# A fused attention and token-mixing kernel: other load queues, a narrower packed tile, fixed buffers, and a new order of all steps

## The chip, the cores and the metric

The kernel runs on one core of one Trainium2 chip. The metric is device time in microseconds (us), the median over runs; lower is better. The core has five instruction queues: TensorE (PE, its weight loads shown apart as PEld), VectorE (DVE), ScalarE (ACT), GpSimd (POOL) and SyncE (SP). Each executes its own instructions strictly in order and waits on semaphores for the others. Transfers are done by 16 DMA engines, fed from a queue of SP, a queue of ACT (both "hardware" queues in the profile) and a queue of POOL (the "software" queue, the only one here that casts fp32 to bf16 on the way).

## The reference

Two attentions in a row and then a token mixer. `B, H, S, Dh = 8, 8, 576, 64`, and 32 packed queries `p` per head.

```python
def sm_attn(qq, kk, vv):
    s = scale * np.matmul(qq, kk.transpose(0, 1, 3, 2))
    s = s - np.max(s, axis=-1, keepdims=True)
    a = np.exp(s)
    a = a / (np.sum(a, axis=-1, keepdims=True) + 1e-09)
    return np.matmul(a, vv)
p_packed = sm_attn(p, k, v)                 # 32 packed rows per head
out = sm_attn(q, p_packed, p_packed)        # every token attends to the 32 rows
x = out.transpose(0, 2, 1, 3).reshape(B, S, H * Dh)
W_tok = scale2 * np.einsum('bsd,btd->bst', x @ w_q, x @ w_k)   # 64 hidden columns
mixed = np.einsum('bst,btd->bsd', W_tok, x)
return np.maximum(mixed, 0.0) @ w_out
```

Inputs and output are fp32; q, k and v are 9.4 MB each.

## The kernel before

The work is cut into 8 batches and each batch into some 30 named steps. A string `ORDER`, written out by hand (or by a planner outside of the file), lists all steps of all batches in one sequence, with `@V`, `@A` or `@P` for the engine that does a step (DVE, ACT, POOL) and `=2,3` for the PSUM banks. A step's instructions are appended to its engine's queue in this sequence, so `ORDER` fixes the order on each engine, but two engines run apart as far as data allow. A place late in `ORDER` does not hold an instruction back if its engine has nothing else to do.

The steps of batch b, with the line of their instructions:

- `LD.kb`, `LD.qb`, `LD.vb`: the casting loads on POOL's queue (L181, L185, L177; v is loaded in two halves). `LD.K0`, `LD.K1` (batch 0's k in fp32, on SP, L163), `LD.P0` to `P3` and `LD.W0`, `W1` (on ACT, L167, L170), `LD.O` (w_out, POOL, L172).
- `KC`, `PC`, `WC` cast k of batch 0, p and the weights on chip (L131, L133, L135 for ACT, POOL, DVE). `KT`, `PX`, `TE`, `PT`, `QV` are transposes in blocks on DVE, all through one helper (L223), told apart by their tiles kT, pT, e, ppT, qT.
- First attention: `S1` scores (PE, L261), `X1` exponential (ACT, L266, tile e1T), `TE`, `PV` (PE, L282, reads v_sb and e), `RC` reciprocal (DVE, L287), `PP` (DVE, L294): divides by the row sum and multiplies by a mask, giving the packed rows pp.
- Second attention: `PT` transposes pp to ppT, `S2` scores (PE, L339), `X2` (ACT, L344), `RS` row sums (DVE, L354), `RR` (DVE, L359), `AM` multiplies (POOL or DVE, L365), `AT` transposes on PE (L374), `AE` evicts them (tile aT).
- Mixer: `QK` multiplies ppT with the weights wqk (PE, L306), `QKE` evicts (tile pqk); `WKQ` (L396, L401), `WE`, `GM` (L422), `GE`, `Y` (L432), `YE`, `MX` (L446) and `MR` (L452, the last 64 tokens), `RL`, `RLF`, `RLR` relu evictions (L457, L459), `OT` (PE, L491) the product with w_out, four matmuls each, `OE`, `OEF` evictions into tiles o and o_rem, `ST`, `STF` stores on SP (L496; L511 for o_rem, the last rows of two batches together).
- `WARM.n` are n matmuls on a zero tile (L535); they compute nothing that is used.

Tiles come from pools (`inpool` 4 buffers, `bpool` 3, `epool` 2, `opool` 10). Each casting load also waits for the one that stands eight DMAs ahead of it on POOL's queue, as they share eight semaphores.

The pp tile of before has 2 x 2 x 128 columns: for each pair of heads the rows stand four times, and the mask leaves one head in each. `PT` turns all of it, so that `QK` can use 128 rows at once.

Of the kernel before, what the change touches and what calls it, by code (L numbers as in the profile page):

```python
# [7 lines left out]
NL, NB, NO, NE = 4, 3, 10, 2  # L8

ORDER = """  # L10
SET.warm LD.P0 LD.P1 LD.P2 LD.P3 LD.W0 LD.W1 LD.K0 LD.k1 LD.K1 SET.mask@V KC.0@V SET.v0@V LD.v0 PC@V
LD.q0 KT.0.0@V KC.1@A SET.v3@V PX@V KT.0.1@V SET.v1@V WARM.27=0 S1.0=0,1,2,3 SET.idf@V KT.1.2@V
SET.aff@P X1.0.1@A LD.k2 WC.0@P SET.aT0@V TE.0.1@V WARM.4=4 S1.1=4,5,6,7 LD.v1 SET.v2@V X1.1.1@A
X1.0.0@A LD.q1 X1.1.0@A TE.0.0@V LD.v2 SET.aT1@V TE.1.1@V WARM.6=2 PV.0.0=2,3 LD.k4 PV.0.1 QV.0.1@V
WC.1@P QV.0.0@V LD.q2 RC.0.1@V RC.0.0@V PP.0.1@V QV.0.2@V PP.0.0@V PT.0@V LD.k3 KT.2.2@V WARM.9=6
S2.0.2=6,7 S2.0.3=0,1 X2.0.2@A X2.0.3@A SET.idb@V TE.1.0@V RS.0.4@V WARM.5=4 PV.1.0=4,5 LD.O PV.1.1
QK.0=2 RC.1.0@V RC.1.1@V RR.0.4@V S1.2=6,7,0,1 PP.1.0@V AM.0.2@P PP.1.1@V AM.0.3@P PT.1@V WARM.1=3
AT.0.2=3 QV.1.1@V AE.0.2@A QK.1=4 X1.2.0@A SET.aT2@V QV.1.0@V QKE.0@A X1.2.1@A QV.1.2@V WARM.2=5
S2.1.3=6,7 LD.v3 QKE.1@A TE.2.1@V S2.1.2=2,3 AT.0.3=5 X2.1.2@A TE.2.0@V X2.1.3@A AE.0.3@V WARM.1=0
PV.2.0=0,1 RS.1.4@V WKQ.0.0=2,3 WKQ.0.2 WKQ.0.1 PV.2.1 WE.0.2@A RR.1.4@V KT.4.2@V AM.1.2@P WARM.1=4  # L20
GM.0=4 AM.1.3@P GE.0@V RC.2.1@V RC.2.0@V WARM.1=6 Y.0=6 PP.2.1@V S1.4=2,3,4,5 YE.0@V PP.2.0@V
X1.4.1@A MX.0.0=6,7 LD.q3 QV.2.0@V MX.0.1=0,1 RL.0.0@A AT.1.3=4 PT.2@V LD.v4 QV.2.1@V AT.1.2=5
X1.4.0@A AE.1.3@V S2.2.3=6,7 RL.0.1@A LD.q4 QV.2.2@V AE.1.2@V S2.2.2=2,3 KT.3.2@V LD.k5 WKQ.1.0=4,5
X2.2.3@A WKQ.1.1 X2.2.2@A WKQ.1.2 S1.3=0,1,6,7 WE.1.2@A RS.2.4@V QK.2=2 X1.3.1@A GM.1=3 LD.q5
OT.0.2=4,5 X1.3.0@A TE.3.1@V GE.1@A OT.0.0=6,7 RR.2.4@V TE.3.0@V OT.0.3 AM.2.2@V AM.2.3@V OT.0.1
LD.k6 OE.0.1@A TE.4.1@V AT.2.2=3 AT.2.3=0 OE.0.0@A AE.2.2@V Y.1=1 TE.4.0@V PV.3.0=4,5 QKE.2@A YE.1@V
MR.0=6,7 PV.3.1 AE.2.3@V RLR.0@A MR.1=2,3 MX.1.0=6,7 LD.v5 RLR.1@A RC.3.1@V QV.3.1@V WKQ.2.0=0,1
RL.1.0@A MX.1.1=2,3 RC.3.0@V WKQ.2.2 PP.3.1@V WKQ.2.1 PP.3.0@V OT.1.4=6 WE.2.2@A PT.3@V QV.3.2@V
QK.3=7 QV.3.0@V OEF.1.4@A GM.2=4 LD.v6 RL.1.1@V PV.4.0=0,1 ST.1.4 GE.2@A QKE.3@A Y.2=6 PV.4.1 YE.2@V
S2.3.2=4,5 S2.3.3=2,3 RC.4.0@V X2.3.2@A RC.4.1@V PP.4.1@V MX.2.0=6,7 OT.1.2=4,5 PP.4.0@V RL.2.0@A  # L30
QV.4.0@V MX.2.1=0,1 X2.3.3@A QV.4.2@V MR.2=6,7 OT.1.3 PT.4@V QV.4.1@V RLR.2@A RL.2.1@A OT.1.0=2,3
RS.3.4@V OE.1.1@A S2.4.2=6,7 S2.4.3=0,1 OT.1.1 RR.3.4@V X2.4.3@A KT.5.2@V AM.3.3@P OT.2.0=4,5
X2.4.2@A OE.1.0@A RS.4.4@V S1.5=0,1,6,7 OT.2.1 LD.q6 X1.5.0@A AM.3.2@V X1.5.1@A LD.k7 AT.3.3=2
RR.4.4@V QV.5.1@V OE.2.0@A OT.2.2=0,1 AM.4.3@P AE.3.3@V QK.4=3 TE.5.1@V AT.3.2=6 OT.2.3 AE.3.2@A
QKE.4@A KT.6.2@V WKQ.3.0=4,5 AM.4.2@P OE.2.1@A AT.4.3=7 LD.v7 WKQ.3.2 WKQ.3.1 AE.4.3@V AT.4.2=6
S1.6=2,3,0,1 WE.3.2@A AE.4.2@V TE.5.0@V WKQ.4.0=6,7 X1.6.1@A QV.5.0@V GM.3=4 LD.q7 WKQ.4.2 X1.6.0@A
WKQ.4.1 GE.3@V PV.5.0=0,1 TE.6.1@V WE.4.2@A Y.3=5 TE.6.0@V PV.5.1 YE.3@A GM.4=4 RC.5.1@V QV.5.2@V
MX.3.1=2,3 RC.5.0@V GE.4@A MX.3.0=6,7 PP.5.0@V RL.3.1@A PV.6.0=4,5 PP.5.1@V Y.4=0 PT.5@V PV.6.1
RL.3.0@A YE.4@V S2.5.3=2,3 RC.6.1@V RC.6.0@V QK.5=1 PP.6.0@V X2.5.3@A PP.6.1@V OT.3.0=6,7 PT.6@V
QKE.5@A S2.5.2=4,5 QV.6.2@V MX.4.0=2,3 QV.6.1@V MR.3=0,1 X2.5.2@A OT.3.1 RL.4.0@A QV.6.0@V RLR.3@V  # L40
S2.6.2=4,5 RS.5.4@V MX.4.1=2,3 S2.6.3=0,1 X2.6.2@A RL.4.1@A OT.3.4=4 X2.6.3@A RR.5.4@V OT.4.0=2,3
OEF.3.4@V AM.5.3@P OE.3.0@A KT.7.2@V QK.6=5 ST.3.4 ST.1.0 OT.4.1 ST.0.0 ST.1.1 ST.0.1 ST.2.0 ST.3.0
OT.3.2=0,1 RS.6.4@V OE.4.0@A AM.5.2@P AT.5.3=4 QKE.6@A ST.4.0 S1.7=6,7,2,3 ST.2.1 RR.6.4@V AE.5.3@V
AT.5.2=5 AM.6.3@P OT.3.3 X1.7.1@A AE.5.2@A X1.7.0@A WKQ.5.0=2,3 OE.3.1@V OT.4.2=4,5 AM.6.2@P WKQ.5.2
WKQ.5.1 QV.7.2@V ST.3.1 TE.7.0@V AT.6.3=6 WE.5.2@A OT.4.3 AE.6.3@V QV.7.1@V GM.5=7 OE.4.1@A
WKQ.6.0=0,1 GE.5@V AT.6.2=6 TE.7.1@V MR.4=2,3 Y.5=7 WKQ.6.1 AE.6.2@A YE.5@A QV.7.0@V WKQ.6.2 RLR.4@A
PV.7.0=4,5 WE.6.2@A MR.5=6,7 MX.5.0=2,3 PV.7.1 RLR.5@V RL.5.0@A MX.5.1=0,1 GM.6=6 RC.7.1@V RC.7.0@V
PP.7.0@V OT.5.4=7 GE.6@A PP.7.1@V RL.5.1@A PT.7@V Y.6=6 OEF.5.4@V S2.7.0=2,3 YE.6@A S2.7.2=4,5
OT.5.2=0,1 X2.7.2@A ST.5.4 ST.4.1 X2.7.0@A RS.7.2@V S2.7.1=6,7 RS.7.0@V MX.6.1=4,5 MX.6.0=2,3
X2.7.1@A OT.5.3 RR.7.2@V RR.7.0@V RL.6.0@A AM.7.2@P RS.7.1@V OT.5.0=6,7 AM.7.0@V OE.5.1@A RR.7.1@V  # L50
RL.6.1@V QK.7=2 AM.7.1@P AT.7.0=3 ST.5.1 OT.5.1 AE.7.0@A QKE.7@V AT.7.2=0 AT.7.1=1 OE.5.0@A AE.7.2@V
WKQ.7.0=4,5 AE.7.1@V MR.6=2,3 WKQ.7.2 WKQ.7.1 ST.5.0 WE.7.0@V OT.6.0=0,1 WE.7.1@A GM.7=6 OT.6.1
GE.7@A RLR.6@A Y.7=7 OT.6.2=4,5 OE.6.0@V YE.7@A MR.7=2,3 MX.7.1=6,7 ST.6.0 MX.7.0=0,1 RLR.7@V OT.6.3
RLF.7.1.0@A RLF.7.0.1@V RLF.7.1.1@A RLF.7.0.0@V OT.7.4=2 OE.6.1@A OT.7.2=3 OEF.7.4@V ST.6.1 OT.7.3=6
ST.7.4 OEF.7.2@V OT.7.1=7 STF.7.2 OEF.7.3@V OT.7.0=0 STF.7.3 OEF.7.1@V STF.7.1 OEF.7.0@A STF.7.0
# [4 lines left out]
def kernel(  # L60
# [42 lines left out]
    inpool = ctx.enter_context(tc.tile_pool(name="inpool", bufs=NL))  # L103
    bpool = ctx.enter_context(tc.tile_pool(name="bpool", bufs=NB))
    epool = ctx.enter_context(tc.tile_pool(name="epool", bufs=NE))
    opool = ctx.enter_context(tc.tile_pool(name="opool", bufs=NO))
# [44 lines left out]
    p32 = opool.tile([P, L * Dh // 2], fp32, tag="o", name="p32")  # L151
    k32 = [epool.tile([P, RQ * Dh], fp32, tag="e2", name="k32") for _ in range(2)]
    w32 = const.tile([P, 2, 2, 2, Dl], fp32)
    wqk = const.tile([P, 2, 2, 3, Dl], bf16)
    wout = const.tile([P, NJ, D], bf16)
    v_bufs = [const.tile([P, 6, W], bf16, name=f"v_sb{n}") for n in range(NL)]
    k_in, q_in = {}, {}

    def load(x):
        a, b = x[0], x[1:]  # L160
        if a == "K":
            x = int(b)
            nc.sync.dma_start(k32[x], pairs(k, 0)[:, x])  # L163
        elif a == "P":
            c = int(b)
            src = p.rearrange("b (i c) (y l) d -> c (b i) y (l d)", i=2, y=2)
            nc.scalar.dma_start(p32[quarter(c)], src[c])  # L167
        elif a == "W":
            w = (moe_w_q, moe_w_k)[int(b)].rearrange("(i c j e) m -> (c j) i (e m)", i=2, c=4, e=2)
            nc.scalar.dma_start(w32[:, int(b)].rearrange("a i e m -> a i (e m)"), w)  # L170
        elif a == "O":
            nc.gpsimd.dma_start(wout, moe_w_out.rearrange("(j a) n -> a j n", a=P))  # L172
        elif a == "v":
            b = int(b)
            for i in range(2):
                src = v[b, 4 * i:4 * i + 4].rearrange("c (g r) d -> g c (r d)", r=R)
                nc.gpsimd.dma_start(v_bufs[b % NL][halves(i), 1:5], src)  # L177
        elif a == "k":
            b = int(b)
            t = k_in[b] = inpool.tile([P, 2, RQ * Dh], bf16, tag="k_sb", name="k_sb")  # L180
            nc.gpsimd.dma_start(t, pairs(k, b))  # L181
        else:
            b = int(b)
            t = q_in[b] = inpool.tile([P, 2, RQ * Dh], bf16, tag="q_sb", name="q_sb")
            nc.gpsimd.dma_start(t, pairs(q, b))  # L185

    idf = const.tile([P, P], fp32)
    warm = const.tile([P, 512], bf16)
    idb = const.tile([P, P], bf16)
    mask = const.tile([P, 4, Dh], bf16)  # L190
    aT_bufs = [const.tile([P, 2, 640], bf16, name=f"aT{n}") for n in range(NB)]

    def setup(n):
# [21 lines left out]
    T = {}  # L215

    def new(key, b, shape, dt=bf16, tag=None, pool=None):
        if (key, b) not in T:
            T[key, b] = (pool or bpool).tile(shape, dt, tag=tag or key, name=key)
# [8 lines left out]
    def KC(x, eng, bk):  # L228
        if 0 not in k_in:
            k_in[0] = inpool.tile([P, 2, RQ * Dh], bf16, tag="k_sb", name="k_sb")  # L230
# [6 lines left out]

    def WC(n, eng, bk):
# [3 lines left out]
        else:  # L242
            copy(eng, wqk[:, :, :, 1], w32[:, 0])
            copy(eng, wqk[:, :, :, 2], w32[:, 0])

    def KT(b, x, eng, bk):
        kT = new("kT", b, [P, 2, RQ, GQ, 2], pool=epool)
        xs = slice(0, 2) if x == 2 else slice(x, x + 1)
        blocks(kT[:, xs].rearrange("a x r g e -> a (x r g e)").bitcast(u32),
               k_in[b][:, xs].rearrange("a x n -> a (x n)").bitcast(u32))  # L250


    def S1(b, eng, bk):
# [314 lines left out]
```

## Time and profile before

| | |
|---|---|
| median of 3 runs | 110.91 us (110.85 to 111.06) |
| span of the profiled execution, first to last instruction | 110.1 us |
| the profiled execution's own time | not given apart from the span |
| busy: PE, DVE, ACT, POOL | 91.8, 87.7, 65.7, 39.0 us |
| PE spent on WARM (L535) | 16.0 us |
| DMA: casting queue (q0), SP's queue (q1), ACT's queue (q10) | 14.09, 10.62, 0.79 MB written |

How to read it. The busy rows of the page cut the span into 40 slices of 2.75 us, a digit is the busy share in tenths; the row PEclk (not shown) gives the clock granted to TensorE. The row GB/s counts bytes written; a casting load writes half of what it reads. A row of a group says line, engine, operation, tiles, count, busy time and mean. "DMA to landing" is the time from the issue of a transfer until its data are there. The chain is followed back from the last instruction, step by step to what released it.

### The profile page before, as it was taken

How to read it: one execution, taken by the hardware profiler on the slowest of the kernel's cores; microseconds unless marked ns; L12 is line 12 of the kernel's file. 1: busy time of each engine (PE TensorE's matmuls, PEld its weight loads, DVE VectorE, ACT ScalarE, POOL GpSimd, SP SyncE). 2: the span in 40 equal slices, each digit the busy share in tenths (PEclk: the TensorE clock that was granted, in tenths of full speed). 3: DMA queues.
4: the chain of work that ended last, by engine and by line, in shares of the span. 5: the costliest groups of instructions: out<-in, count | busy, mean ns of one | idle time of the engine just before them, and what ended most of it. 6: DMA issues, size and time to landing. Idle time of an engine off the chain costs nothing.

```text
span 110.1 us, 3454 instructions
## 1 busy us (share of the span) xinstructions
PE 91.8 (83%) x1465; PEld 50.8 (46%) x1481; DVE 87.7 (80%) x170; ACT 65.7 (60%) x97; POOL 39.0 (35%) x53
## 2 busy tenths in 40 slices
PE   5992079869486778999999999899999999999940
PEld 2340022445264365565635577644567654654410
DVE  3310995999999997999998999998979779839630
ACT  0062025022473599398699979899874998846220
POOL 3070049940843972424006892000853002300000
PEclk9999656999999999999999999999999999999999
DMA  3999999999999999999999999999999998362594
GB/s 105 334 257 230 214 199 143 185 206 203 214 213 207 210 205 215 204 208 217 209 252 210 204 207 215 210 207 210 242 406 406 394 405 338 134 266 92 213 381 174
DMA packets 13167, 25.71 MB, mean 234 GB/s; under 512 B 992, under 2 KB 6112, under 8 KB 13152
## 3 DMA queue, kind: packets, MB, share of 16 engines
q0 software_dynamic: 8960, 14.09, 71.4%
q1 hardware_dynamic: 3456, 10.62, 25.1%
q10 hardware_dynamic: 736, 0.79, 2.5%
q8 instruction: 11, 0.18, 0.6%
q14 instruction: 4, 0.03, 0.1%
HBM read 30.15 MB, written 9.44 MB: 360 GB/s over the span
## 4 chain that ended last, share of the span: by engine, by line
PE 42%; DVE 26%; ACT 13%; DMA 7%; issue 5%; ACTq 2%; POOL 1%; DVEq 0%; POOLq 0%
PE ps L491 21%; DMA p<-in_p_dram 7%; DVE e L223 6%; ACT relu L457 5%; DVE kT L223 5%; DVE rs L354 4%; ACT e L344 3%; PE ps L339 3%; PE ps L282 3%; PE ps L446 2%; PE ps L374 2%; ACT e1T L266 2%; DVE qT L223 2%; DVE pp L294 2%; DVE aT L135 2%
## 5 line engine op out<-in xcount | busy, mean ns | idle before, releaser
L491 PE MATMUL ps<-wout,relu 128*128 128x512 bf16 x120 | 30.0, 379 | 0.7 <-issue 0.3
L365 POOL TENSOR_TENSOR a<-e,rr 128x256 bf16<-128x256 f32 (+2 forms) x13 | 16.0, 1244 | 35.1 <-DVE rr L359 14.9
L457 ACT ACTIVATE relu<-ps 128x1024 bf16<-128x1024 f32 (+1 forms) x14 | 17.1, 1242 | 1.8 <-PE ps L446 1.4
L535 PE MATMUL ps<-warm 128*128 128x512 bf16 x52 | 16.0, 449 | 1.6 <-DVE warm L138 1.2
L491 PEld LDWEIGHTS <-relu 128*128 128x128 bf16 x128 | 11.4, 98 | 12.1 <-issue 1.4
L131 ACT ACTIVATE o<-ps 128x1024 f32<-128x1024 f32 (+1 forms) x13 | 12.8, 996 | 6.5 <-PE ps L491 6.5
L266 ACT ACTIVATE e1T<-ps 128x576 bf16<-128x576 f32 x16 | 9.9, 661 | 11.0 <-PE ps L261 8.7
L344 ACT ACTIVATE e<-ps 128x256 f32<-128x256 f32 (+2 forms) x17 | 11.0, 675 | 6.1 <-PE ps L339 5.9
L354 DVE TENSOR_REDUCE rs<-e 128x40 f32<-128x1280 f32 (+2 forms) x10 | 12.1, 1209 | 1.6 <-ACT e L344 1.5
L177 POOL DMA_DIRECT2D v_sb<-in_v_dram x16 | 10.1, 634 | 8.8 <-DVE v_sb L206 4.0
L223 DVE STREAM_TRANSPOSE e<-e1T 128x576 bf16<-128x576 bf16 x16 | 11.9, 756 | 1.3 <-ACT e1T L266 1.2
L223 DVE STREAM_TRANSPOSE qT<-q_sb 128x512 uint32<-128x512 uint32 (+1 forms) x24 | 12.7, 549 | 0.0
L223 DVE STREAM_TRANSPOSE kT<-k_sb 128x1152 uint32<-128x1152 uint32 (+1 forms) x9 | 10.9, 1207 | 0.0
L535 PEld LDWEIGHTS <-warm 128*128 128x128 bf16 x57 | 5.8, 110 | 9.6 <-issue 4.9
L261 PE MATMUL ps<-kT,pT 32*32 32x288 bf16 x256 | 5.0, 328 | 5.2 <-DVE pT L223 4.8
L339 PE MATMUL ps<-ppT,qT 64*128 64x64 bf16 x320 | 7.3, 190 | 2.1 <-DVE ppT L223 1.1
L282 PE MATMUL ps<-v_sb,e 64*64 64x192 bf16 x288 | 8.6, 247 | 0.5 <-DVE e L223 0.4
L131 ACT ACTIVATE wkq<-ps 128x896 bf16<-128x896 f32 (+1 forms) x8 | 7.0, 878 | 3.0 <-PE ps L401 3.0
L339 PEld LDWEIGHTS <-qT 64*128 64x128 bf16 x320 | 6.1, 94 | 5.7 <-issue 2.5
L374 PE MATMUL ps<-idb,a 128*128 128x128 bf16 x80 | 6.8, 220 | 1.0 <-POOL a L365 1.0
L282 PEld LDWEIGHTS <-e 64*64 64x64 bf16 x288 | 6.0, 106 | 2.9 <-DVE e L223 1.8
L294 DVE SCALAR_TENSOR_TENSOR pp<-ps,rec,mask 128x256 bf16<-128x256 f32 x16 | 7.1, 478 | 0.3
(58 smaller groups left out, 126.4 us busy)
## 6 DMA issues: line engine op xcount, KB each, us to landing
out_dram<-o SPq DMA_DIRECT2D x14, 512.0 KB, 4.5
v_sb<-in_v_dram POOLq DMA_DIRECT2D x16, 288.0 KB, 11.7
q_sb<-in_q_dram POOLq DMA_DIRECT2D x8, 576.0 KB, 12.3
k_sb<-in_k_dram POOLq DMA_DIRECT2D x7, 576.0 KB, 13.7
k<-in_k_dram SPq DMA_DIRECT2D x2, 576.0 KB, 5.1
out_dram<-o_rem SPq DMA_DIRECT2D x4, 256.0 KB, 3.6
out_dram<-o SPq DMA_DIRECT2D x4, 256.0 KB, 2.7
p<-in_p_dram ACTq DMA_DIRECT2D x4, 128.0 KB, 7.9
```

The source lines that it names most:

```text
L131: nc.scalar.activation(o, i, COPY)
L177: nc.gpsimd.dma_start(v_bufs[b % NL][halves(i), 1:5], src)
L223: nc.vector.transpose(o, i)
L266: nc.scalar.activation(e1T[:, cc], T["s1", b][cc], EXP, scale=scale)
L282: nc.tensor.matmul(T["pv", b][halves(cc), i, cc * Dh:(cc + 3) * Dh], lhsT, rhs, start=n == 0, stop=n == R - 1, skip_group_check=True)
L339: nc.tensor.matmul(ps[:, y, t - t0, i], lhsT, rhs, start=e == 0, stop=e == 1)
L344: nc.scalar.activation(e2[:, t0:t1].rearrange("a t (i y n) -> a y (t i) n", i=2, y=2), T["s2", b, c].rearrange("a y t i n -> a y (t i) n") ...
L354: nc.vector.tensor_reduce(rs[:, t0 * H:t1 * H], e2v(b, c), axis=AX, op=ADD)
L365: e.tensor_tensor(a2[:, t0:t1].rearrange("a t i (u l) -> a (t i u) l", l=L), e2v(b, c), T["rr", b][:, t0 * H:t1 * H].to_broadcast((P, (t1 ...
L457: nc.scalar.activation(o, i, RELU)
L491: nc.tensor.matmul(ps, lhsT, wout[:, j, :], start=j == 0, stop=j == NJ - 1)
L535: nc.tensor.matmul(ps, warm[:, 0:P], warm, start=True, stop=True)
```

## The change

Queues of the start: batch 0's k comes on SP and ACT at once (K1 first on SP, K0 first on ACT), p in two quarters on each, the weights on SP. In the casting queue q and v of batch 0 come first, then k, q, v of batch 1, of batch 2 and so on. `KC.0` is done by POOL, one `WC` by ACT, the third `WC` copy is gone.

pp holds a head pair once (2 x 2 x 64 columns); `PP`, `PT` and the copy in `QKE` get half or two thirds as wide; `QK` is done as two halves of 64 rows; a new step `QD` (POOL or DVE) doubles the 64 query columns in pqk that `QK` no longer delivers twice.

All pools are replaced by fixed buffers that are used in turn (three, two or four of a kind, and six o tiles that hold a whole batch instead of ten that hold half of one). The scratch tiles of the start (k32, p32, w32, idf) lie in the e2 and o buffers. kT is laid out with 64 columns per row so that `S1` and `TE` read runs of 32.

`ORDER` is new throughout: order of steps, engines of some, places of loads and stores. WARM has 87 matmuls instead of 57. `DIAG` is empty and `TURN` holds all batches, so the branches for them are never taken or always.

```diff
-NL, NB, NO, NE = 4, 3, 10, 2
+NL, NB, NO, NE = 4, 3, 6, 2
+DIAG = ()
+TURN = tuple(range(8))
 ORDER = """
-SET.warm LD.P0 LD.P1 LD.P2 LD.P3 LD.W0 LD.W1 LD.K0 LD.k1 LD.K1 SET.mask@V KC.0@V SET.v0@V LD.v0 PC@V
-LD.q0 KT.0.0@V KC.1@A SET.v3@V PX@V KT.0.1@V SET.v1@V WARM.27=0 S1.0=0,1,2,3 SET.idf@V KT.1.2@V
...
-OEF.3.4@V AM.5.3@P OE.3.0@A KT.7.2@V QK.6=5 ST.3.4 ST.1.0 OT.4.1 ST.0.0 ST.1.1 ST.0.1 ST.2.0 ST.3.0
...
+SET.warm@V LD.K1@S LD.P1@S LD.K0@A LD.P0@S LD.W1@S LD.P3@A LD.P2@A SET.v0@V SET.v1@V SET.mask@V
+SET.aT0@V SET.idf@V LD.q0 LD.v0 SET.aff@P LD.k1 SET.v2@V LD.W0@S LD.q1 LD.v1 KC.0@P KT.0.0@V KC.1@A
+KT.0.1@V PC@V PX@V LD.k2 LD.q2 LD.v2 WC.0@P QV.0.1@V QV.0.0@V WC.1@A QV.0.2@V WARM.31=4 S1.0=0,1,2,3
+X1.0.1@A X1.0.0@A TE.0.1@V TE.0.0@V WARM.11=4 PV.0.0=0,1 PV.0.1 RC.0.0@V RC.0.1@V PP.0.1@V PP.0.0@V
+PT.0@V KT.1.2@V WARM.6=2 S2.0.3=4,5 S2.0.2=0,1 X2.0.2@A X2.0.3@A WARM.5=6 S1.1=0,1,2,3 QK.0=4
+RS.0.4@V QKE.0@A X1.1.0@A X1.1.1@A SET.aT1@V TE.1.0@V RR.0.4@V QV.1.1@V TE.1.1@V AM.0.2@V QD.0@P
+SET.idb@V QV.1.0@V WARM.18=5 PV.1.0=2,3 PV.1.1 AM.0.3@P LD.k3 SET.v3@P LD.O QV.1.2@V RC.1.1@V
...
+GM.0=0 X1.2.1@A GE.0@A X1.2.0@A RS.1.4@V RR.1.4@V AM.1.3@P AM.1.2@P LD.q3 LD.v3 LD.k4 LD.q4 TE.2.1@V
...
+QKE.4@A YE.3@A OT.2.3 MX.3.0=4,5 MR.3=6,7 OE.2.1@A RLR.3@A PV.5.0=2,3 PV.5.1 MX.3.1=0,1 RL.3.0@V
+LD.q6 LD.v6 LD.k7 AM.4.2@P LD.q7 AM.4.3@P LD.v7 RC.5.1@V RC.5.0@V QD.4@V PP.5.0@V PP.5.1@V PT.5@V
+QV.5.2@V QV.5.0@V QV.5.1@V AT.4.2=6 AE.4.2@A RL.3.1@A OT.3.4=4 S1.6=2,3,6,7 AT.4.3=5 OT.3.0=0,1
+AE.4.3@V X1.6.1@A X1.6.0@A OEF.3.4@A TE.6.1@V TE.6.0@V S2.5.3=6,7 S2.5.2=2,3 X2.5.2@A WKQ.4.0=4,5
...
+AE.5.3@V S2.6.2=4,5 QK.6=2 QKE.6@V KT.7.2@V RL.4.1@A RL.4.0@A S2.6.3=6,7 WKQ.5.0=2,3 X2.6.2@A
+X2.6.3@A WKQ.5.1 WKQ.5.2 OT.4.0=0,1 S1.7=4,5,6,7 OT.4.1 WE.5.2@A X1.7.0@A X1.7.1@A GM.5=2 OT.4.2=4,5
+OE.4.0@A GE.5@A OT.4.3 RS.6.4@V RR.6.4@V TE.7.1@V TE.7.0@V QV.7.1@V Y.5=2 PV.7.0=0,1 QD.6@P AM.6.3@P
+AT.6.3=6 AM.6.2@P AT.6.2=7 YE.5@V QV.7.0@V AE.6.3@V AE.6.2@V QV.7.2@V OE.4.1@A MR.4=2,3 MX.5.0=4,5
+PV.7.1 RC.7.1@V RC.7.0@V RLR.4@A RL.5.0@A ST.0.0 ST.0.1 ST.1.4 ST.3.4 ST.2.1 ST.1.1 ST.3.1 ST.1.0
+ST.3.0 ST.2.0 ST.4.1 ST.4.0 PP.7.0@V PP.7.1@V PT.7@V WKQ.6.0=2,3 WKQ.6.1 WKQ.6.2 MR.5=6,7 MX.5.1=0,1
...
     def KT(b, x, eng, bk):
-        kT = new("kT", b, [P, 2, RQ, GQ, 2], pool=epool)
+        kT = new("kT", b, [P, 2, R, 2 * GQ, 2], bufs=NE)
...
     def TE(b, cc, eng, bk):
-        e1 = new("e1", b, [P, R, C, 2, L], pool=epool)
+        e1 = new("e1", b, [P, R, C, 2, L], bufs=NE)
         blocks(e1[:, :, cc].rearrange("a r x l -> a x r l"),
-               T["e1T", b][:, cc].rearrange("a x (t r g) -> a x r g t", t=2, r=R))
+               T["e1T", b][:, cc].rearrange("a x (r m) -> a x r m", r=R))
...
     def PP(b, i, eng, bk):
-        pp = new("pp", b, [P, 2, 2, 2 * Dh])
...
+        pp = new("pp", b, [P, 2, 2, Dh])
+        nc.vector.scalar_tensor_tensor(pp[:, i], T["pv", b][:, i, Dh:3 * Dh].rearrange("a (x d) -> a x d", x=2),
+                                       T["rec", b][:, i], mask, op0=MULT, op1=MULT)
...
     def QK(b, eng, bk):
-        ps = T["qk", b] = bank(bk, [2, 3 * Dl])
+        ps = T["qk", b] = bank(bk, [2, 2 * Dl])
         for i in range(2):
             for e in range(2):
-                nc.tensor.matmul(ps[:, i], T["ppT", b][:, i, :, :, e].rearrange("a c l -> a (c l)"),
-                                 wqk[:, i, e].rearrange("a x m -> a (x m)"), start=e == 0, stop=e == 1)
+                for y in range(2):
+                    nc.tensor.matmul(ps[halves(y), i],
+                                     T["ppT", b][halves(y), i, :, :, e].rearrange("a x l -> a (x l)"),
+                                     wqk[halves(y), i, e].rearrange("a x m -> a (x m)"),
+                                     start=e == 0, stop=e == 1, skip_group_check=True)
...
+    def QD(b, eng, bk):
+        w = T["pqk", b]
+        copy(eng, w[:, :, 2 * Dl:], w[:, :, Dl:2 * Dl])
```

The order of the casting loads, from both versions of `ORDER`:

```
before: k1 v0 q0 k2 v1 q1 v2 k4 q2 k3 O v3 q3 v4 q4 k5 q5 k6 v5 v6 q6 k7 v7 q7
after:  q0 v0 k1 q1 v1 k2 q2 v2 k3 O q3 v3 k4 q4 v4 k5 k6 v5 q5 q6 v6 k7 q7 v7
```

In the program of after, SP's first stores wait for the evictions that they store and for old DMAs alone; no store waits for a load.

## The prediction

> **What bounds the kernel now.** First the slices of the page, for the engines and the DMA.
>
> ```profile
> PE   5992079869486778999999999899999999999940
> DVE  3310995999999997999998999998979779839630
> DMA  3999999999999999999999999999999998362594
> GB/s 105 334 257 230 214 199 143 185 206 203 214 213 207 210 205 215 204 208 217 209 252 210 204 207 215 210 207 210 242 406 406 394 405 338 134 266 92 213 381 174
> ```
>
> DVE is full from slice 8 (22 us) to slice 27, PE from slice 15 (41 us) to the end. DMA is full from the first microseconds to slice 28 at some 210 GB/s (the casting loads count by the bf16 that they write), then drains the outputs at 406. The stretches of 2 us give the edges.
>
> ```profile
> 16.00:18.00 2.00, 2.00 (x37) 0.45 (x36) 1.71 (x5) 0.24 (x1) 2.00 (x5) 0.50 0.79 101
> 76.00:78.00 2.00, 1.95 (x11) 0.96 (x11) 1.63 (x4) 2.00 (x3) 1.11 (x1) 1.00 1.08 206
> 80.00:82.00 2.00, 1.95 (x50) 1.19 (x49) 1.39 (x4) 1.54 (x5) 1.00 (x1) 1.00 1.01 407
> ```
>
> The last two columns are DMA share and GB/s. One dip (16 to 18, half of 2 us lost: 1.05 us), loads to 78, then stores alone at 407. SyncE's timeline says why the two are apart:
>
> ```profile
> 52.02 26.05 SPq L511 DMA_DIRECT2D out_dram<-o_rem  x2
> 78.16 10.08 SPq L496 DMA_DIRECT2D out_dram<-o  x9
> ```
>
> ST.3.4 heads the line of stores: SyncE waits 25 us for that o_rem, and every L496 store starts behind it, after the loads. The DMA answer for the last issues, and the chain around the end:
>
> ```profile
> q_sb<-in_q_dram POOLq DMA_DIRECT2D x1, 576.0 KB, 13.4
> v_sb<-in_v_dram POOLq DMA_DIRECT2D x1, 288.0 KB, 11.3
> 86.53 0.54 PE ps L282 x20
> 100.52 5.30 PE ps L491 x24
> 105.84 0.60 ACT o L131
> ```
>
> q7 is issued at 66.14 and lands at 79.5, the second half of v7 at 76.8. PV.7.0, the first user of v7, begins at 86.46: the loads are full-time, but 10 us ahead of need. From 79 on the chain is PE without a break to 105.8, then one eviction and the last store: 110.1. So before is bound by DVE up to about 78 and by PE behind it, with DMA a full but not yet deciding third.
>
> **The change, by parts.** The profiled span is 110.1 us, and the median of the runs 110.91; the page gives no other time for that execution, so I add 0.8 to a span. What a measurement here can tell from no change is about 0.2% (the runs lie 0.19% apart).
>
> *Work per engine, all of it cheaper or moved.* PP halves from 128x256 (478 ns): between 239 and 478, taken 270 (the DVE copy of 128x128 from PSUM is 252), so 16 x 0.21 = 3.3 us less on DVE. PT halves to 128x128 uint32; the qT row of that shape is 288 against 435: 8 x 0.15 = 1.2 less. DVE also loses KC.0 (0.76), three 128x1024 aT copies (2.0), the aT copy of 128x256 (0.4), AM work (1.21 + 0.68, getting back 2 x 0.40), evictions (0.69 + 1.36), a GE and a YE (0.65), one v memset (0.54); it gains an RL (1.27) and three QD of 128x128 bf16 (idb's 183 ns each: 0.55). Sum: about 10 us off 87.7. ACT gains the three aT copies (1.03 each by the o row), small ones (0.6 + 0.6 + 1.2 + 0.3 + 0.4 + 0.4), gives one RL (1.33) and 0.1 per QKE: +4.5 on 65.7. POOL gains KC.0 (421 ns for 256 columns, so 1.9 for 1152; 1.6 at the least), AM 1.9 + 1.05 - 1.2, five QD (0.2 to 0.4 each), a memset: about +5 on 39. TE now reads 32 neighbours where it read a permuted run, KT writes in steps of 8 bytes: 0 to -0.1 us on each of 16 TE (756 ns for 576 elements; kT needs 750 for as many of uint32), and 0 on KT, since QV writes in such steps at the same pace. I take 0 for both. QK: eight matmuls of 64 rows and 128 columns for four of 128 and 192 (about 0.5 us a group); PV's 36 on 64 rows take 0.94, 26 ns each, so 0.2 to 0.4: -0.2 per batch. Pools against fixed buffers: no instruction, the same number of each, nothing. WARM goes from 57 to 87, 30 x 0.21 = 6.4 us on PE, in gaps before 45 us; uncovered, up to 2 us at the start if the granted clock is at 0.5 as in 12 to 18 us.
>
> *The start.* P's last quarter lands at 10.83 behind both k halves; the chain then has pbf 0.69, kT 0.69, a v memset 0.54, PX 0.90. With P in two queues and kT and memset out of the way S1.0 can come at 11 to 12.6 instead of 13.9. PV.0 then needs v0, second in the casting queue: as many bytes stand before it as before the second half of v0 now (15.2). PT.0 ends at about 17.5 to 19 against 23.6. But batch 1's k is now third in that queue (where q0 lands now, 17.9, was 11.2) and v1 comes at about 23.6: PT.1 near 26 against 29.1, PT.2 near 35 against 38.5. A lead of 3 us is left in this stage, because the casting loads set the pace, 2.85 us each (k2 at 21.1 to q7 at 79.5: 58.4 us for 19 loads, wout at 3.5 and an o_rem).
>
> *The stores.* This is what I think decides. The new SP order is ST.0.0, ST.0.1, ST.1.4, ST.3.4, ST.2.1, ST.1.1, ST.3.1, ST.1.0, ST.3.0, ST.2.0. Their place in the list of steps is late (after RL.5.0), but SyncE executes nothing else and waits for data alone. So the first three (1.31 MB) go when batch 0's and 1's outputs exist, 41 to 55 us, in the thick of the loads. ST.3.4 is again a gate, but opens sooner: OEF.3.4 now stands on ACT ahead of X2.5 and behind little more than PV.5. v5 lands now at 65.5; in the new order q5 comes after it (-2.85), the dip goes (-1.05), the o_rem of 52 (-0.65) is replaced by 1.31 MB (+3.2): 64.2. PV.5, MX.3.1, AT, OT.3.4, on ACT RL.3.1 (1.33) and two X1 (1.3) lead to a gate at about 69. Then six stores of 512 KB and the o_rem (3.4 MB) run against v6, k7, q7, v7.
>
> What a store does to loads beside it, the one time that it happens now, 56 to 58 us:
>
> ```profile
> q0 software_dynamic: 130, 0.29, 74.9%
> q1 hardware_dynamic: 110, 0.20, 30.8%
> ```
>
> The shares add up as without a store (loads alone show 108 to 112%): DMA time taken by the store is taken from the loads. So the last load lands at: 79.5 - 1.05 - 0.65 = 77.8 for the loads alone (no gap left: AM.0.3 and AM.1 stand before k3 and q3 in POOL's queue; from PT.0 at 18 and PT.1 at 26 it takes S2, X2, RS, RR and AM some 6 to 7 us each, so they end at 25 and 33, while the loads issued before them last to 32 and 38), plus ten stores, 8 x 0.524 + 2 x 0.262 = 4.72 MB at 407 GB/s = 11.6: 89.4 us for v7. Two values for what is served before v7: by time share, the row gives the store 30.8 / 105.7 = 29%; 12 us of loads left at 69 then need 17 us, v7 at 86. By turns, 110 store packets went for 130 load packets; a store of 4 KB rows has 128 packets of about 148 ns (16 engines x 2 us over the 218 packets of 80 to 82 us), so about 900 store packets pass before the 1600 of the loads, v7 at 89.4. I take the turns, since the small share comes from that store's 2 KB rows, and keep 86 for the range. [...]
>
> *Who waits.* KT.7.2 (k7, now near 82 instead of 73.9) stands in DVE's queue ahead of RS.6.4 and TE.7; PV.7.0 stands on PE ahead of AT.6, MR.4, MX.5 and all later OT. So PE stops, and nothing covers it. From PV.7.0 on, before needs 110.1 - 86.46 = 23.6 us, PE full. The new order leaves more behind PV.7.0: AT.6 (0.56), MR.4 (0.17), WKQ.6 (0.9), less QK (0.2): +1.4. Fourteen OT are behind it in both. End: 89.4 + 23.6 + 1.4 = 114.4; with 0.8, **115.2**. The saved 10 us of DVE are then spent waiting for k7, q7 and v7; what is late next, behind those, is PE.
>
> **The rivals.**
> *A, the stores squeeze in and PE decides (faster).* If v6 to v7 keep ahead of need, count PE from PV.5: it starts when v5 lands, 64.2 to 64.7, and is done near 65.7. In the old order PE took from PV.5.1 (69.0) to 105.84, 36.8 us; the new order has AT.4, S1.6 and WKQ.4 more behind that point (0.56 + 0.48 + 0.9) and MX.3.0, MR.3 and three times QK's 0.2 less (0.3 + 0.2 + 0.6), so 37.6: 103.3, and 4.3 for eviction and store: 107.6, with 0.8 108.4. For it: PE is full from 41 us, and DVE has 10 us to give. Against it: DMA has no free microsecond before 78. It decides if v7 lands before about 84.
> *B, the full gain.* DMA never binds, DVE's relief shows: 104 to 105. Needs the loads to go faster than 2.85 us each; no stretch shows it.
> *C, the time share.* v7 at 86: 86 + 25.0 + 0.8 = 111.8. Speaks for it the row above taken literally.
> *D, more waits on top.* A gate in DVE's queue (KT.7.2 before RS.6.4) delays AM.6 and WKQ.6 too, or WARM runs at a granted clock of 0.5 before PV.0 (11 x 0.21 more): 117 to 118.
> That the interleaving of p, k and weights lands nothing earlier is possible too; it costs at most the 1.3 to 3 us of the start, and the sum above does not hang on it.
>
> **How the numbers follow.** Likeliest, v7 near 89: 115.2, chance 0.48. C 0.16, D 0.12, A 0.16, B 0.05, something at no change 0.03. Range: from just under A (108.2) to the middle of D (117.6); left out are B, half of D and the far half of A, some 0.19. Faster by over 0.2%: A and B, 0.21; same 0.03; slower 0.76. The likeliest case's own range is 113 to 117.
>
> **What would show it.** Right: DMA busy with loads up to 86 to 90 us, SP's stores (L546 in the new file) from about 41 us and in a row from about 69; PE idle before the L282 matmuls of batch 7, with v_sb as releaser, DVE idle before a kT at about 78 to 82; DVE busy 76 to 79 us; PP near 270 ns, PT near 290. Wrong: v7 landing before 84 us, or PE full from 66 us on; or SyncE's first store later than the last load, in which case A or B holds.

## The result, and the profile after

The changed kernel takes 119.46 us (median of 4 runs, 118.96 to 120.01), the kernel before 110.98: a ratio of 1.076 (95% interval 1.072 to 1.080). The profiled execution of the changed kernel took 118.96 us, its span is 117.2. The prediction was 115.2, in a range to 117.6: the direction held, and the time fell outside. Some executions take over 1.5% longer than the fastest of the same kernel; the times below leave them out, and of the one run whose profile is such an execution (the three early stores moved) only the transfers and the granted clock are read.

The slices of the page for the changed kernel (2.93 us each):

```profile
PE   5994999999999969986899999799304999999920
DVE  5349668988977999793999999998700599556040
PEclk9999999999999999999999999999965699999999
DMA  3999999999999999999999999999998000354792
GB/s 69 391 267 215 216 212 205 213 216 201 218 201 214 203 214 289 297 210 250 211 210 210 212 207 227 291 293 318 322 355 337 22 6 0 144 214 157 288 369 90
```

PE and DVE, full to the end before, now stand nearly still in slices 28 to 30 (counted from 0, 82 to 91 us), and the clock granted to PE falls there. The 407 GB/s of stores that had followed the loads are gone. Instead the loads run to 90 us at 290 to 350 GB/s, with stores mixed in. SyncE's timeline shows the stores, the chain of waits the last load (its second column is the time from issue to landing), and PE's timeline what waits for it:

```profile
40.49 2.85 SPq L546 DMA_DIRECT2D out_dram<-o  x2
49.57 19.72 SPq L544 DMA_DIRECT2D out_dram<-orem  x2
69.34 34.08 SPq L546 DMA_DIRECT2D out_dram<-o  x10
```

```profile
65.58 23.93 DMA v_sb<-in_v_dram
89.56 1.01 PE ps L309 x19
```

```profile
82.69 0.30 PE L463 MATMUL ps<-pp,g 64*64 64x128 bf16 x4
85.63 0.24 PE L309 MATMUL ps<-v_sb,e 64*64 64x192 bf16 x1 [2.64 <-DMA v_sb<-in_v_dram]
89.56 1.01 PE L309 MATMUL ps<-v_sb,e 64*64 64x192 bf16 x19 [3.69 <-DMA v_sb<-in_v_dram]
```

The first three stores go at 40 and 49 us, the gate ST.3.4 opens at 69.3, and ten L546 stores follow. The second half of v7 lands at 89.5 us. PE does one matmul of PV.7.0 in the 6.6 us before 89.56. The stretches of 2 us around that point (PE busy, ..., granted clock, DMA share, GB/s):

```profile
84.00:86.00 2.00, 0.24 (x1) 0.10 (x1) 0.14 (x1) 0.00 (x0) 0.00 (x0) 1.00 1.10 324
86.00:88.00 2.00, 0.00 (x0) 0.00 (x0) 0.00 (x0) 0.00 (x0) 0.00 (x0) 0.53 1.08 368
88.00:90.00 2.00, 0.44 (x13) 0.44 (x16) 0.00 (x0) 0.00 (x0) 0.00 (x0) 0.50 0.96 383
90.00:92.00 2.00, 2.00 (x31) 1.39 (x23) 0.42 (x1) 0.00 (x0) 0.00 (x0) 0.50 0.30 121
92.00:94.00 2.00, 2.00 (x38) 1.36 (x38) 1.39 (x7) 1.71 (x2) 0.00 (x0) 0.77 0.00 0
```

So the tail, from PV.7.0 to the end, begins at half clock. It also ends later: DVE does the last eviction at 112.18, and the span ends 5.0 us behind PE (112.16 to 117.2), against 4.3 before.

### The profile page after: what moved, and what is told of

It is laid out like the page before. It is cut to its first block, busy times and chain, and to the rows that moved or that the text cites. A ratio compares the mean times of both kernels' runs of the same rounds, so it can differ in the third digit from the quotient of the medians.

```text
span 117.2 us, 3579 instructions
## 1 busy us (share of the span) xinstructions
PE 97.4 (83%) x1524; PEld 53.8 (46%) x1543; DVE 83.5 (71%) x163; ACT 70.1 (60%) x106; POOL 43.7 (37%) x58
## 4 chain that ended last, share of the span: by engine, by line
DMA 50%; PE 21%; DVE 9%; POOL 8%; issue 5%; ACT 2%; POOLq 0%; DVEq 0%; ACTq 0%
DMA v_sb<-in_v_dram 36%; DMA q_sb<-in_q_dram 14%; PE ps L526 11%; POOL v_sb L177 3%; POOL q_sb L183 3%; PE ps L309 2%; PE ps L478 2%; PE ps L405 2%; PE ps L370 2%; POOL a L396 1%; DVE rs L385 1%; ACT e L375 1%; DVE relu L491 1%; DVE kT L231 1%; DVE pp L318 1%
## 5 line engine op out<-in xcount | busy, mean ns | idle before, releaser
L396 POOL TENSOR_TENSOR a<-e,rr 128x1024 bf16<-128x1024 f32 (+2 forms) x13 | 18.1, 1408 | 28.9 <-DVE rr L390 21.9
L572 PE MATMUL ps<-warm 128*128 128x512 bf16 x81 | 21.3, 401 | 1.8 <-DVE warm L138 1.2
L489 ACT ACTIVATE relu<-ps 128x1024 bf16<-128x1024 f32 (+1 forms) x13 | 15.3, 1227 | 1.4 <-PE ps L478 1.4
L309 PE MATMUL ps<-v_sb,e 64*64 64x192 bf16 x288 | 9.5, 258 | 7.3 <-DMA v_sb<-in_v_dram 7.2
L385 DVE TENSOR_REDUCE rs<-e 128x40 f32<-128x1280 f32 (+2 forms) x10 | 11.9, 1201 | 2.2 <-ACT e L375 2.2
L572 PEld LDWEIGHTS <-warm 128*128 128x128 bf16 x87 | 8.2, 102 | 11.0 <-issue 2.1
L309 PEld LDWEIGHTS <-e 64*64 64x64 bf16 x288 | 6.8, 112 | 10.7 <-issue 8.3
L133 POOL COPY pqk<-pqk 128x128 bf16<-128x128 bf16 x5 | 1.6, 329 | 21.5 <-ACT pqk L131 19.1
L135 DVE COPY aT<-ps 128x128 bf16<-128x128 bf16 (+1 forms) x8 | 3.4, 440 | 8.6 <-PE ps L405 8.6
L131 ACT ACTIVATE aT<-ps 128x128 bf16<-128x128 bf16 (+2 forms) x9 | 5.3, 601 | 5.7 <-PE ps L405 5.7
L489 ACT ACTIVATE rem<-ps 128x256 bf16<-128x256 f32 x5 | 1.9, 383 | 9.9 <-PE ps L484 9.9
```

The source lines that it names most:

```text
L131: nc.scalar.activation(o, i, COPY)
L309: nc.tensor.matmul(T["pv", b][halves(cc), i, cc * Dh:(cc + 3) * Dh], lhsT, rhs, start=n == 0, stop=n == R - 1, skip_group_check=True)
L385: nc.vector.tensor_reduce(rs[:, t0 * H:t1 * H], e2v(b, c), axis=AX, op=ADD)
L396: e.tensor_tensor(a2[:, t0:t1].rearrange("a t i (u l) -> a (t i u) l", l=L), e2v(b, c), T["rr", b][:, t0 * H:t1 * H].to_broadcast((P, (t1 ...
L489: nc.scalar.activation(o, i, RELU)
L572: nc.tensor.matmul(ps, warm[:, 0:P], warm, start=True, stop=True)
```

## The experiments

**The stores.** The theory: stores that run beside the last loads push v7 back, and nothing else of the change costs time. The rivals: the start, the narrow tile or the order cost it; or any stores beside loads cost the same, wherever they stand. First, all stores are held back by an output that is evicted late.

```diff
-ST.0.0 ST.0.1 ST.1.4 ST.3.4 ST.2.1 ST.1.1 ST.3.1 ST.1.0 ST.3.0 ST.2.0 ST.4.1 ST.4.0
+ST.4.1 ST.0.0 ST.0.1 ST.1.4 ST.3.4 ST.2.1 ST.1.1 ST.3.1 ST.1.0 ST.3.0 ST.2.0 ST.4.0
```

> The changed kernel with one difference: SP's first store is ST.4.1, whose data exist only near 80 us, so that all other stores stand behind the loads. Theory 1 (every byte stored before v7 pushes v7 by its DMA time): ten stores, 4.72 MB, 11.6 us leave the load phase, v7 lands at 77 to 79 instead of 89.5, PE no longer stops before PV.7.0, its clock stays at 1, and the span falls from 117.2 to 104 to 108, below before's 110.1. Theory 2 (the new order and the moved steps are slower by themselves, ACT +4.5 us, 30 more WARM matmuls): the span stays above 113, whatever v7 does.

112.35 us, 7.1 less than as written, 1.012 (1.007 to 1.017) of before. v7 lands at 77.6 us, PE stands still for less than 1 us from 62 us on and ends at 103.0, where rival A of the prediction had 103.3. But the span is 110.6 and not 104 to 108: SyncE's timeline has the gate at 82.8, and DMA idles from 78 us till then:

```profile
82.81 2.12 SPq L546 DMA_DIRECT2D out_dram<-o  x3
```

```profile
80.00:82.00 2.00, 2.00 (x26) 0.94 (x28) 1.89 (x3) 1.41 (x4) 2.00 (x2) 1.00 0.00 0
84.00:86.00 2.00, 2.00 (x53) 1.38 (x49) 1.91 (x8) 1.75 (x3) 0.00 (x0) 1.00 1.00 389
```

By an estimate, all 9.4 MB of output at about 0.4 MB/us need 23.6 us from there, to 106.4 (the last bytes move at 108), and the span ends 7.6 us behind PE, 2.6 more than as written: now the stores set the end. Too late a gate costs as well.

Next, only the three early stores are moved behind ST.3.4:

```diff
-ST.0.0 ST.0.1 ST.1.4 ST.3.4 ST.2.1 ...
+ST.3.4 ST.0.0 ST.0.1 ST.1.4 ST.2.1 ...
```

> The changed kernel with ST.3.4 first in SP's queue, so that ST.0.0, ST.0.1 and ST.1.4 (1.31 MB) start at about 69 us with the others instead of from 40 us. Theory 1 in its strict form (only the sum of bytes before v7 counts): v7 lands within 0.7 us of 89.5 and the time is the same within 1%. Rival (it is the place that counts: early stores delay the middle batches, or late ones collide with v loads in short packets): the time moves by more than 1.5 us, either way.

1.0125 of before (1.006 to 1.019), from 112.34 and 112.56 us, 7.0 less than as written. The same bytes stand on SP's queue, yet v7 lands earlier (chain of waits):

```profile
64.44 20.48 DMA v_sb<-in_v_dram
```

At 84.9, 4.6 us earlier, with DMA then busy with stores to 91 us, as in the kernel as written. So not all queued stores pass ahead of v7 here. What v7's date follows is the bytes of stores that do pass. From 40 us to v7's landing SP's queue moved 3.26 MB here, 5.40 MB in the kernel as written, and nothing with all stores held back, where v7 lands at 77.6. The delays against that run, 7.3 and 11.9 us, are 2.2 us for each MB in both, whether the stores stand early or late. How many pass is a matter of turns. From 74 to 86 us the queues of the kernel as written moved (packets, MB, share of the 16 engines; q1 is SP's queue, q0 that of the casting loads):

```profile
q1 hardware_dynamic: 733, 2.60, 58.1%
q0 software_dynamic: 730, 1.09, 49.9%
```

That is one store packet for one load packet. With the three stores moved, 1.46 MB of loads are left from 69 us on, against 2.11 MB as written, so the loads are through before the stores are. The strict form of theory 1 missed, since it took all queued bytes as passing ahead of v7; the turns that the prediction had chosen over the time share of 29% hold.

The counter-test puts early stores into the kernel before:

```diff
-PV.4.0=0,1 ST.1.4 GE.2@A ... QK.6=5 ST.3.4 ST.1.0 OT.4.1 ST.0.0 ST.1.1 ST.0.1 ST.2.0 ST.3.0 ... ST.2.1
+PV.4.0=0,1 ST.0.1 ST.0.0 ST.1.4 GE.2@A ... QK.6=5 ST.1.1 ST.1.0 ST.2.0 ST.2.1 ST.3.4 OT.4.1 ST.3.0 ...
```

> The kernel before, with only the order of its stores changed: ST.0.0, ST.0.1 ahead of ST.1.4 and ST.1.0, ST.1.1, ST.2.0, ST.2.1 ahead of ST.3.4, so that six stores (3.15 MB) run from about 47 us on beside the loads. Theory 1: 3.15 MB at 407 GB/s are 7.7 us; v7 lands at 84 and q7 at 87 instead of 76.8 and 79.5, 3 to 4 us after the first QV.7 (83.06) and later than KT.7's and QV.6's dates as well: span 113 to 115 against 110.1. Theory 2 (stores are harmless, the new order is at fault): no change within 1 us.

118.97 us, 1.071 (1.066 to 1.076): a loss as large as that of the change, in the old kernel, by store order alone. The span of 117.4 us lies beyond the 113 to 115 expected. SyncE's timeline, PE's, and a stretch:

```profile
58.20 7.84 SPq L497 DMA_DIRECT2D out_dram<-o  x4
```

```profile
68.09 0.49 PE L262 MATMUL ps<-kT,pT 32*32 32x288 bf16 x32 [2.33 <-DVE kT L224]
72.83 1.01 PE L283 MATMUL ps<-v_sb,e 64*64 64x192 bf16 x19 [1.61 <-DMA v_sb<-in_v_dram]
```

```profile
72.00:74.00 2.00, 1.17 (x32) 1.17 (x35) 0.00 (x0) 0.00 (x0) 0.00 (x0) 0.50 1.20 207
```

The loads come late in the middle already, PE stops at 66 us, and its clock is at half for most of 68 to 80: 0.50 in that stretch, and 32 matmuls of L340 take 1.03 us at 78.0 and 0.66 at 82.6. How much of the loss is the clock's was not separated here.

**The clock.** In the kernel as written, 32 WARM matmuls are put ahead of PV.7.0, so that PE does not stand still while it waits:

```diff
-... QV.7.1@V Y.5=2 PV.7.0=0,1 ...
+... QV.7.1@V Y.5=2 WARM.32=0 PV.7.0=0,1 ...
```

> The changed kernel with 32 idle matmuls in front of PV.7.0 (6.8 us at 0.213 each), where PE waits for v7 from 83 to 89.5 us. v7 still lands at 89.5. If the granted clock of 0.5 between 86 and 93 us comes from PE's pause, the clock stays at 1 there and the tail from v7 to the end falls from 27.7 to about 25.7: time -1.8 us. Rival (the tail is long for its work and its waits, not for the clock): no change within 0.5 us.

118.03 us against 119.46, 1.4 less where 1.8 was expected. The clock stays at 1:

```profile
88.00:90.00 2.00, 2.00 (x11) 0.75 (x10) 0.00 (x0) 0.00 (x0) 0.00 (x0) 1.00 0.97 386
```

PV.7.0 starts at 90.0, 0.4 us later (the WARM overshoots), and PE ends 21.3 us behind it instead of 22.6. The fallen clock is worth 1.3 us of the tail.

**A gate between.** ST.3.0's output is evicted at 73.2 us, so it makes a gate at 73:

```diff
-ST.0.0 ST.0.1 ST.1.4 ST.3.4 ST.2.1 ST.1.1 ST.3.1 ST.1.0 ST.3.0 ST.2.0 ...
+ST.3.0 ST.0.0 ST.0.1 ST.1.4 ST.3.4 ST.2.1 ST.1.1 ST.3.1 ST.1.0 ST.2.0 ...
```

> The changed kernel with ST.3.0 as the first store of SP's queue, and then the order of the change. ST.3.0 waits for the eviction OE.3.0, which ended at 73.2 us with the stores held back, so it opens the gate at about 73 us instead of 40 (as written) or 82.8 (held back by ST.4.1). Theory (stores that run beside the last loads push v7 back, and only that): little of the loads is left at 73 us, v7 lands at 79.5 to 81.5, PV.7.0 waits 0 to 0.5 us, PE is full to about 103.3, the stores are through by 104, and the end is set by PE: span 106.5 to 107.5, time 108 to 109.3, faster than before. Rival (any row of 512 KB stores beside the last loads costs as much as in the kernel as written): v7 at 84 or later, PV.7.0 waits 2.5 us or more with the clock falling, time 111.5 or more.

109.80 us, 0.987 (0.984 to 0.991): 1.3% under before, 9.7 us less than as written, by the place of one name in a list. Timelines of SyncE and PE:

```profile
73.53 2.20 SPq L546 DMA_DIRECT2D out_dram<-o  x3
```

```profile
81.91 0.27 PE L309 MATMUL ps<-v_sb,e 64*64 64x192 bf16 x2
82.01 0.59 PE L309 MATMUL ps<-v_sb,e 64*64 64x192 bf16 x18
```

The stores issued from 73.5 us on move their first packets only from 76 us, when 0.15 MB of the loads are left. 1.39 MB of stores pass ahead of v7, which lands at 80.1, 1.8 us later for each MB. So a MB of stores costs v7 about as much here as elsewhere; what differs is that fewer pass ahead of it, and that v7 has until 82 us. PV.7.0 waits for nothing (no bracket), PE ends at 103.3 as expected, 5.0 us ahead of the end. The time is 0.5 over the range expected, which had 3.2 to 4.2 us behind PE instead of 5.0.

**The other parts, on top of that gate.** Each of the next three undoes one.

```diff
+pp, ppT, mask, wqk and QK as before (256 columns), no QD     (wide tile)
+LD.P0@A to LD.P3@A, LD.W0@A, LD.W1@A, LD.K0@S, LD.K1@S       (old hardware queues)
+casting queue: k1 v0 q0 q1 v1 ... for q0 v0 k1 q1 v1 ...      (k1 first)
```

> The kernel with the gate at 73 us, and in it the packed tile of before: PP over 256 columns, PT over 256, QK as four matmuls of 192 columns, no QD (pp and ppT in two buffers instead of three, to fit). DVE gets 16 x 0.13 + 8 x 0.12 = 3.1 us more and loses three QD of 0.75. Theory (up to 62 us the casting loads set the pace, behind that PE, so the narrow tile is worth nearly nothing): 0 to 0.5 us over the kernel with the gate at 73. Rival (the narrow tile shortens PV, PP, PT, S2 in each batch, and that carries to the end): 8 x 0.38 = 3 us over it. Third (QD, 0.75 us on DVE and on the chain at 40 us, costs more than the narrow tile saves): 0.3 to 1 us under it.

> The kernel with the gate at 73 us, and in it the hardware queues of before: p in four quarters and the weights on ACT, batch 0's k on SP. P's last quarter lands at 10.8 instead of 9.4, S1.0 comes at 13 instead of 11. Theory (the casting loads set the pace of batches 1 to 7): the 1.5 to 2 us at the start are gone by batch 2, 0 to 0.4 us over the kernel with the gate at 73. Rival (the start carries through): 1.5 us or more over it.

> The kernel with the gate at 73 us, and in it the first three casting loads in the order of before (k1, v0, q0 for q0, v0, k1). v0 comes at the same place, q0 at about 18 instead of 12, k1 earlier. Theory: PV.0 starts as now, S2.0 one to two us later, S1.1 no later than now; from batch 2 on the loads set the pace: within 0.4 us of the kernel with the gate at 73. Rival (batch 0's lead carries): 1 us or more over it.

Wide tile 111.35, old hardware queues 111.93, k1 first 117.57 us. The narrow tile is worth 1.5 us, between the two theories; PV.4 starts at the same time in both (54.0), so it comes behind that, in batches 5 to 7. For the start the rival is right: 2.1 us, 1.8 of them already at PV.0 (16.45 for 14.65) and still there at PV.3 (46.90 for 45.10). k1 first costs 7.8, on the rival's side (1 us or more), and DVE's timeline shows why it is so much:

```profile
16.68 1.50 DVE L231 STREAM_TRANSPOSE qT<-q_sb 128x512 uint32<-128x512 uint32 x3 [5.81 <-DMA q_sb<-in_q_dram]
```

QV.0 waits for q0, and TE.0, which the whole of batch 0 needs, stands behind it on DVE. The test is to move QV.0 behind PT.0:

```diff
-... PX@V ... QV.0.1@V QV.0.0@V WC.1@A QV.0.2@V ... TE.0.1@V TE.0.0@V ... PT.0@V
+... PX@V ... WC.1@A ... TE.0.1@V TE.0.0@V ... PT.0@V QV.0.1@V QV.0.0@V QV.0.2@V
```

> The kernel with the gate at 73 us, with k1 first in the casting queue and q0 third as in the run that took 117.6 us, and QV.0 moved behind PT.0 on DVE, so that TE.0 and PV.0 do not stand behind the wait for q0. Theory (the 7.8 us of that run are QV.0's wait in DVE's queue ahead of TE.0): PV.0 back at about 15, S2.0 at 18.5 to 19.5, time 1.5 to 2.5 us over the kernel with the gate at 73. Rival (the place of q0 in the casting queue costs it in any case): 4 us or more over it.

111.81 us: 5.8 of the 7.8 were that wait in the queue, 2.0 are q0's place among the loads. The fixed buffers, the 30 more WARM matmuls and the rest of the new order were not tested apart.

**A copy on the chain.** With the gate at 73 the chain of the front runs through DVE, and QD.2 on it takes 1.8 us for a copy of 128x128. It goes to ACT, with QD.1 and QD.4, and the identity's cast goes ahead of PC:

```diff
-QD.1@V ... QD.2@V ... QD.4@V ... SET.idb@V QV.1.0@V
+QKE.1@A QD.1@A ... QKE.2@A QD.2@A ... QKE.4@A QD.4@A ... SET.idb@V PC@V
```

> The kernel with the gate at 73 us, and in it QD.1, QD.2 and QD.4 on ACT right behind their QKE instead of on DVE (one of them lies on the chain at 40 us with 1.8 us), and the cast of the identity (0.45 us on the chain at 24 us) ahead of PC, where DVE waits for p. Theory now (batches 0 to 4 are a chain through DVE's queue in order, and what it saves in front reaches the end, while the loads follow): 1.5 to 2.2 us under the kernel with the gate at 73, 107.6 to 108.3. Rival (the casting loads set the pace of the front half, as the prediction had it): within 0.4 us of it.

109.19 us, 0.6 less: between the two. PV.3 starts 0.95 earlier (44.15 for 45.10), and not 1.8, since PE's OT.0 is next on the chain of waits:

```profile
38.35 2.91 PE ps L526 x12
```

QD.4 on ACT then stands on the chain with 0.3; that it costs this was not tested alone. The same edit in the kernel with the stores as written:

> The changed kernel with its stores as written, and the same move of QD to ACT and of the identity's cast. Theory (the stores between the loads set when v7 lands, 89 us, and the end hangs on that): the front is 1.5 to 2 us earlier, the gate too, but v7 lands within 1 us of 89.5, and the time stays at 118.5 to 119.7. Rival (the front carries through here too): 117 to 118.

119.73 us, no gain, but not quite as expected: the gate opens no earlier (69.8), since the front's gain ends at v4, which the early stores make late too. PV.3 starts 0.8 us earlier than as written (43.77 for 44.53), and PV.4 then waits for v4, which lands at 55.1 us (54.8 as written). PE's timeline:

```profile
55.16 0.93 PE L309 MATMUL ps<-v_sb,e 64*64 64x192 bf16 x35 [1.62 <-DMA v_sb<-in_v_dram]
```

v7 lands at 90.1.

**The fastest version.** ST.3.0 first in SP's queue (the gate opens at 71.5 here), QD.1 and QD.2 on ACT, QD.4 back on DVE, and no WARM ahead of PV.2:

```diff
-MR.0=2,3 WARM.4=5 PV.2.0=4,5 PV.2.1
+MR.0=2,3 PV.2.0=4,5 PV.2.1
```

> The kernel with the gate at 73 us and QD.1, QD.2 on ACT, with QD.4 back on DVE (on ACT it lay on the chain at 61 us with 0.3) and without the four WARM matmuls ahead of PV.2 (1.0 us on the chain at 32 us; TE.2, which PV.2 needs, is done 0.9 us earlier). Theory (the front is a chain, what leaves it reaches the end): 0.6 to 1.2 us under the kernel with the three QD on ACT, 108.0 to 108.6. Rival (DVE's QV.2 and the later PE work fill the place, or the clock falls without the WARM): within 0.3 us of it.

108.14 us, 0.973 (0.969 to 0.977), 1.05 less than the version above; its two edits were not tested apart. The chain now holds the landing of v2 (14.31 + 17.74 = 32.05 us), which PV.2 waits for, and PV.7.0 starts at 80 us, where v7 lands: loads and PE bind together, so a shorter front should not help much further, which was not tested. Last, the one store that the change put on ACT's queue goes back to SP's:

```diff
-STF.7.2@A
+STF.7.2
```

> The fastest kernel so far (108.1 us), with the last store, STF.7.2, on SP's queue behind STF.7.1 instead of on ACT's queue. Theory (a store lands 0.5 us later and issues 0.1 us longer on ACT's queue): PE's end to the end of the span in 4.3 to 4.5 us instead of 5.0, 0.5 to 0.7 us under it, 107.4 to 107.7. Rival (SP's queue with its three other stores just ahead costs the same, or the landing is only late because of what runs beside it): within 0.2 us of it.

108.16 us: no difference. The last store lands 3.2 us after its issue on either queue (2.6 before), so the queue is not what lengthens the end.

## Why the prediction was wrong

The mechanism, its place and its date were right; the tail behind v7 and the constant around the span were too small. Of the 3.8 us between 115.2 and the profiled 118.96 (the median of 119.46 lies 0.5 above that execution):

- *The gate and v7*: forecast 69 and 89.4, measured 69.3 and 89.5 (0.2 us to PV.7.0). The turns behind it were right too, with 733 store packets for 730 of the loads. That the date fits to 0.2 us is in part luck: 5.40 MB of stores passed ahead of v7 and not 4.72, at 2.2 us for each MB and not 2.46 (1 MB at 407 GB/s), from 77.6 us for the loads alone and not 77.8.
- *The tail, "23.6 + 1.4 = 25.0"*, failed: 27.6. PE took 22.6 instead of 20.8 from PV.7.0. 1.3 of that is the granted clock, at half after PE had stood still; rival D named a clock at 0.5, but at the start, and the likeliest case assumed a full one. 0.5 is the term "+1.4" for the work that the new order leaves behind PV.7.0: at a full clock PE takes 21.3 us with the WARM, 21.4 with the stores held back and 21.4 with the gate at 73, where the sum had 20.8. Which item of that term is too small stays open. The other 0.8 lie behind PE's end: 0.1 is the eviction on DVE (0.69 for 0.60), 0.6 the landing of the last store; ACT's queue is excluded as its cause, and what it is stays open.
- *The 0.8 us around the span* failed: the runs show 1.8 in both kernels (118.96 and 117.2; 110.52 and 108.7). By that, before's profiled span of 110.1 belongs to an execution of about 111.9 us, longer than the median that I set beside it. That is 1.0 us.

0.2 + 2.6 + 1.0 = 3.8. The range ended at 117.6 because rival D had the only upward term; neither of the two that failed had a bound.

Rival A was right in what it says of PE: with v7 in time PE ends at 103.0 to 103.3. PV.7.0 is then reached at 81 to 82, so v7 has to land by there, not by 84. What A lacked was the store order. C's time share is excluded by v7's date and by the packets, and B never came.

The work per engine was off. DVE is busy for 83.5 us, not 76 to 79:

```profile
L318 DVE SCALAR_TENSOR_TENSOR pp<-ps,rec,mask 128x128 bf16<-128x128 f32 x16 | 4.9, 347 | 0.3
L135 DVE COPY pqk<-pqk 128x128 bf16<-128x128 bf16 x3 | 2.2, 746 | 0.0
```

PP at 347 ns instead of 270 gives back 2.1 us instead of 3.3. The three QD take 2.2 instead of 0.55, and AM on DVE grew by 0.9 us (3.6 for 2.7) where 1.1 less were counted. KC.0 on POOL was cheaper, 1.15 us for 1.9. That none of it shows in the time as written, because PE and DVE wait for v4 and v7, is argued; the run with QD on ACT and the stores as written, which gained nothing, speaks for it.

The start came a little earlier than forecast (S1.0 at 10.8, PT.0 at 16.1, PT.1 at 25.6, PT.2 at 34.6). The reason given for its small worth, "the casting loads set the pace", is wrong where the stores stay out of the way: undone on top of the later gate, the old hardware queues cost 2.1 us, from PV.0 to the end. With k1 first the loads moved only 94 to 147 GB/s from 29 to 43 us, against 210 else: the loads followed the front, not the front the loads. In the kernel as written the stores make the loads late, so that they do bind, at v4 and at v7.

## What to carry to other kernels

A store's place in a list of steps says nothing on when it runs; what it waits for does. When one queue of stores has a gate, treat the gate's time as a parameter: here 40 and 69, 68, 73 and 82.8 us gave 119.5, 112.5, 109.8 and 112.4 us for the same work. Count the bytes of stores that pass ahead of a load, packet for packet while both queues have some (733 for 730 here), and set the load's date against the date of its first use. And when a forecast lets an engine stand still, price its clock behind the pause (1.3 us of the tail here), and look how the profiled span stands to the runs before adding a constant.

## What the runs showed of the hardware

*The clock.* PE paused from 83 to 89.5 us with one matmul in between, and the granted clock was 0.53 from 86 and 0.50 from 88, back at 1 only by about 93; with WARM in the pause it stayed at 1 (1.00 from 84 to 94). In this trace it took 3.1 us from the pause's start to the fall and 3.4 us of work to the return. The run with the three early stores moved has other times: its clock (1.00 from 80 to 82, 0.50 from 84 to 90, 0.84 from 90 to 92) fell at 83.8, 1.9 us after PE had stopped, and was back at 90.6, after 5.7 us of work. The mean granted clock of its four executions is 0.960, 0.973, 0.998 and 0.999, so in two of them the clock hardly fell; how long PE paused in those is not on record.

*DVE beside POOL.* The same copy of 128x128 bf16 on DVE took 0.17 us and 1.90 us within one execution (DVE's timeline, then POOL's):

```profile
33.44 0.17 DVE L135 COPY pqk<-pqk 128x128 bf16<-128x128 bf16 x1
39.87 1.90 DVE L135 COPY pqk<-pqk 128x128 bf16<-128x128 bf16 x1
```

```profile
39.64 2.08 POOL L396 TENSOR_TENSOR a<-e,rr 128x1024 bf16<-128x1024 f32 x1 [2.32 <-DVE rr L390]
```

The long one ends with POOL's multiply, within 0.1 us, and POOL starts 0.2 us ahead of it. That POOL's instruction is the cause was not tested by itself.
